# Batches 2 and 3 of an attention: keys and queries transposed by VectorE in 32x32 blocks in place of TensorE

## The chip, the cores and the metric

The kernel runs on one core of one Trainium2 chip. The metric is the time of one execution on the device in microseconds (us). The engines are TensorE (PE; its weight load is PEld), VectorE (DVE), ScalarE (ACT), GpSimd (POOL) and SyncE (SP), which issues nearly all transfers. Each engine works through its own queue in order. Sixteen data engines move what SP issues.

## The reference

A sparse attention, and then a block that mixes by Fourier transforms and applies a dense layer of two matrices. All is float32. The attention, cut to what matters here:

```python
batch, n_heads, seq, head_dim = (4, 8, 768, 64)
k_sum = k.reshape(B, H, nb, block, D).max(axis=3)          # block = 32, nb = 24
scores_l = scale * np.matmul(q, k.transpose(0, 1, 3, 2))
mask_l = np.abs(pos[:, None] - pos[None, :]) < window      # window = 16
scores_s = scale * np.einsum('bhsd,bhnd->bhsn', q, k_sum) + np.log(block)
# softmax over [scores_l where mask_l, scores_s], times [v, mean of v over each block]
```

Then `x`, the heads side by side (4, 768, 512), goes through `u = x + real(fft(fft(x, axis=1), axis=2))`, a normalisation of each row, and `u + relu(un @ w_ch1) @ w_ch2` with 512 x 2048 and 2048 x 512 weights (given as float64).

## The kernel before

The two heads of a pair are worked on together: a group `(b, g)` is batch `b` and head pair `g` (four groups a batch). For scores, keys and queries must stand with the head's 64 dimensions on the partitions: rows 0 to 63 for the first head, 64 to 127 for the second, and the 768 tokens along the row. These are the tiles `kt` (keys, two buffers, with 16 columns of margin on each side) and `qt` (queries).

**Loading.** `load(b, g)` (line 574) fetches the keys and the queries of a group, each as one transfer on SP, into a tile tagged `nat` (named `kn` or `qn`, four buffers, that is two groups). Tokens stand on the partitions: a partition has two neighbouring tokens for each of three blocks of 256 and for each head, in runs of 512 bytes. `gen_attention` loads three groups ahead (`n3`), once the group one ahead has been prepared.

**Preparing.** `prepare(b, g)` (line 678) turns these tiles. For batches 1 to 3 each tile takes six TensorE transposes of 128x128 through `ident` (line 699) into two PSUM tiles `qk`, and four ScalarE copies (line 701) of 64 partitions x 384 that write every second column of `kt` or `qt`. Then VectorE takes the maxima of the 24 blocks of keys into `km` (line 706).

**Attention.** `scores` (line 765) multiplies `kt` and `qt` block by block into `sc`, ScalarE takes the exponential (line 771), VectorE applies the mask `near`. `sum_scores` (line 781) does the same against `km`. `values` (lines 788 to 810) multiplies with the values `vw` (loaded by `load_narrow_values` as four transfers of 64 partitions, in runs of 256 bytes) and divides.

**The dense part.** `gen_hidden(b, c)` runs the first matrix in a seven-product scheme: for each of eight `j`, products into the banks `hx`, `hy`, `hz` (line 1268), gathered in `h` by ScalarE copies and VectorE sums (all VectorE sums have line 566, as they go through the helper `tt`). `gen_out` does the second matrix (lines 1310 and 1333). The weights are converted once during batch 0 (tile `words`), kept in HBM as `dw1` and `dw2`, and fetched again for each later batch (`w<-dw`). In batch 1, `get_w2` fetches four parts of each of the first four `w2` tiles, builds the other three by VectorE sums (`w<-w`), and stores them.

**Order.** The attention of batch `b + 1` is woven into the dense part of batch `b`: `drive` advances the generators `most` and `gen_attention(b + 1)` in a fixed ratio, and the scheduler then fixes each engine's queue from priorities and modelled times. The last group's preparation of batch 1's attention is that of group (2, 0). `marks["dense"]` is the dense VectorE sum that was emitted last, and

```python
with tc.issue_after(marks["dense"]):
```

puts what is emitted inside behind it in VectorE's queue. `fetch` keeps SP's queue in program order only while `in_order[0]` is true, which ends before batch 0's dense part.

Of the kernel before, what the change touches and what calls it, by code (L numbers as in the profile page):

```python
# [490 lines left out]
def _main_program(ctx, tc, q, k, v, moe_w_ch1, moe_w_ch2, out):  # L491


    nc = tc.nc
    B, H, S, D = q.shape
# [55 lines left out]
    def fetch(out, in_):  # L551

        ins = nc.sync.dma_start(out=out, in_=in_)
        if in_order[0]:
            tc.keep_in_program_order(ins)

    def abank(shape, name):
        return psum.tile(shape, FP, tag="attn", bufs=4, name=name)

    def bank(shape, name):  # L560
        return psum.tile(shape, FP, tag="bank", bufs=4, name=name)
# [10 lines left out]
    nat, marks = {}, {}  # L572

    def load(b, g, *which):

        for n in which or (1, 0):
            t = nat[b, g, n] = apool.tile([P, 2, NST // 2, 2 * D], FP, tag="nat", bufs=4, name=f"{'qk'[n]}n_{b}_{g}")
            fetch(out=t.rearrange("p e j n -> p (e j) n"),
                  in_=(q, k)[n][b, 2 * g:2 * g + 2].rearrange("e (j p s) d -> p (e j) (s d)", p=P, s=2))

# [97 lines left out]
    def prepare(b, g, *which):  # L678
        qn, kn = (nat[b, g, n] for n in range(2))
        kt, km = kt_bufs[g % 2], km_bufs[g % 2]  # L680
        qt = apool.tile([P, S], FP, tag="qt", name=f"qt_{b}_{g}") if 0 in (which or (0,)) else None
        for n in which or (1, 0):
            src, dst = (kn, kt[:, W:W + S]) if n else (qn, qt)
            if is_wide(b):
                for j0, j1 in ((0, 2), (2, 3)):
                    n = 2 * P * (j1 - j0)
                    ps = bank([P, n], f"qk_{b}_{g}_{j0}")
                    for j in range(j0, j1):
                        for s in range(2):
                            for e in range(2):  # L690
                                nc.tensor.matmul(ps[D * e:D * (e + 1), 2 * P * (j - j0) + s:2 * P * (j - j0 + 1):2],
                                                 src[:, e, j, D * s:D * (s + 1)], ident, start=True, stop=True)
                    nc.scalar.copy(out=dst[:, 2 * P * j0:2 * P * j1], in_=ps)
            else:
                for e in range(2):

                    ps = abank([P, S2], f"qk_{b}_{g}_{e}")
                    for j in range(NST // 2):
                        nc.tensor.transpose(ps[:, P * j:P * (j + 1)], src[:, e, j, :], ident)  # L699
                    for s in range(2):  # L700
                        nc.scalar.copy(out=dst[D * e:D * (e + 1), s:S:2], in_=ps[D * s:D * (s + 1)])
        if which == (0,):
            nat[b, g] = qt
            return
        with tc.issue_after(marks["fold", 0]) if (b, g) == (1, 0) else ExitStack():
            nc.vector.tensor_reduce(out=km[:, 0:nb], in_=kt[:, W:W + S].rearrange("p (n f) -> p n f", f=BLOCK),
                                    op=ALU.max, axis=AX.X)
        nat[b, g] = qt
# [110 lines left out]
    def first_attention():  # L819
# [3 lines left out]
        wt["fold"] = split_fold(0, fold)  # L823
        p = {0: wide_scores(0, 0, lambda: add_blocks(0))}
        prepare(0, 1)
        sum_values(0, 0)
        load(0, 3)
        for g in range(NP - 1):
            p[g + 1] = wide_scores(0, g + 1, (lambda: add_blocks(1)) if g == 1 else None)
            wide_values(0, g, p[g], x)  # L830
            load_values(*following(0, g, 2))
            for par in range(2):
                fold_sequence(par, g)
            if g == 0:
                get_tables(0)
            if g < NP - 2:
                prepare(0, g + 2)
                sum_values(0, g + 1)
            if g == NP - 3:
                load_raw(1)  # L840
                load(1, 0)
                load_raw(2)
                sum_values(0, g + 2)
# [105 lines left out]
    def gen_attention(b):  # L949
# [3 lines left out]
        for g in range(NP + 1):  # L953
# [26 lines left out]
            if n1 and b == 1:  # L980
                prepare(*n1)
            elif n1:
                prepare(*n1, 1)
                for _ in range(pause // 2):
                    yield
                prepare(*n1, 0)
            if n3:
                load(*n3)
# [400 lines left out]
    for vw in vw_bufs:  # L1389
        nc.gpsimd.tensor_copy(out=vw[:, :, D].rearrange("p (e n) -> p e n", e=2),  # L1390
                              in_=count[:, None, :].to_broadcast([P, 2, NQ]))
# [115 lines left out]
```

## Time and profile before

| | |
|---|---|
| median of three runs | 814.2 us (813.47 to 815.4) |
| the profiled execution | 820.64 us, its span 818.8 us |
| mean granted TensorE clock | 0.981 |
| TensorE busy | 793.2 us, 97% |
| VectorE busy | 492.6 us, 60% |
| ScalarE busy | 252.0 us, 31% |
| GpSimd busy | 46.2 us, 6% |
| SP's transfer queue (q1) | 100992 packets, 118.52 MB, 50.2% of 16 engines |

The profile is one execution, taken by the hardware profiler, 6.4 us above the median of the runs without it. The page gives for each engine the busy time, then the span in 40 slices of 20.5 us with the busy tenths of each (and the granted clock of TensorE, PEclk), then the chain of work that ended last, followed back from the last instruction. The groups name line, engine, operation, output and inputs with their shape, the count, busy time, mean duration, and the idle time of the engine just before them with what ended it. "issue" is time in which an engine waited for nothing that the profile shows. The share of the data engines can exceed 1[...].

### The profile page before, as it was taken

What the parts mean: (1) busy time and instruction counts of PE and PEld (TensorE: products, weight loads), DVE (VectorE), ACT (ScalarE), POOL (GpSimd) and SP (SyncE); (2) the same over time, 40 slices, a digit from 0 to 9 for tenths busy, and PEclk for the clock granted to TensorE, in tenths of its full rate; (3) what the DMA queues carried; (4) which work ended last, traced back from release to release, by engine and by line L of the source; (5) the groups of instructions that cost most, each with busy time, mean ns of one, the idle gap of its engine ahead of it and who ended that gap; (6) DMA issues with size and microseconds to landing.
All of it is one profiled execution on the core that took longest, in us unless ns stands there. A gap on an engine that the chain in (4) does not pass through costs nothing.

```text
span 818.8 us, 14635 instructions
## 1 busy us (share of the span) xinstructions
PE 793.2 (97%) x5998; PEld 581.6 (71%) x5998; DVE 492.6 (60%) x1121; ACT 252.0 (31%) x549; POOL 46.2 (6%) x85
## 2 busy tenths in 40 slices
PE   8969899999999999999999999999999999999997
PEld 6768665545579865688669876688659875786686
DVE  5767999887997753453577723364566723532351
ACT  3523765543635132411126114320116202001200
POOL 0010000000000310000030300000120000000000
PEclk9959999999999998999999999999999999999999
DMA  9998699788734376744614256411614044205001
GB/s 201 229 207 172 161 311 295 169 260 249 248 135 145 116 256 157 169 116 103 251 42 149 78 194 185 92 47 35 243 39 152 26 160 163 90 1 224 1 27 54
DMA packets 102332, 121.85 MB, mean 149 GB/s; under 512 B 50768, under 2 KB 83760, under 8 KB 102064
## 3 DMA queue, kind: packets, MB, share of 16 engines
q1 hardware_dynamic: 100992, 118.52, 50.2%
q0 software_dynamic: 576, 2.10, 0.8%
q8 instruction: 49, 0.80, 0.4%
q10 hardware_dynamic: 688, 0.20, 0.1%
q14 instruction: 27, 0.22, 0.1%
HBM read 97.22 MB, written 23.59 MB: 148 GB/s over the span
## 4 chain that ended last, share of the span: by engine, by line
PE 89%; DVE 4%; ACT 3%; DMA 2%; issue 1%; SPq 0%; DVEq 0%
PE hx L1268 20%; PE ox L1333 17%; PE hz L1268 10%; PE oz L1333 8%; PE o L1310 5%; PE hy L1268 5%; PE oy L1333 4%; PE y L1168 4%; PE sc L765 2%; PE mx L1127 2%; PE unt L1246 1%; PE av L798 1%; PE qk L699 1%; PE av L803 1%; PE ss L781 1%; DMA words<-in_v_dram 1%
## 5 line engine op out<-in xcount | busy, mean ns | idle before, releaser
L1268 PE MATMUL hx<-u,w 128*128 128x384 f32 x512 | 187.1, 493 | 0.3 <-ACT h L1279 0.2
L1268 PEld LDWEIGHTS hx<-u,w 128*128 128x128 f32 x512 | 95.1, 191 | 68.1 <-issue 3.6
L1268 PE MATMUL hz<-u,w 128*128 128x384 f32 x256 | 93.8, 489 | 0.0
L1333 PE MATMUL oz<-w,s 128*128 128x256 f32 x336 | 80.8, 379 | 0.0
L1333 PE MATMUL ox<-w,s 128*128 128x256 f32 x336 | 80.3, 380 | 0.0
L1333 PE MATMUL ox<-w,h 128*128 128x256 f32 x336 | 79.0, 380 | 1.0 <-DVE x L566 1.0
L566 DVE TENSOR_TENSOR x<-ox,x 128x256 f32<-128x256 f32 x84 | 35.2, 422 | 68.5 <-PE ox L1333 68.1
L1268 PEld LDWEIGHTS hz<-u,w 128*128 128x128 f32 x256 | 48.9, 192 | 34.6 <-issue 1.1
L1333 PEld LDWEIGHTS ox<-w,h 128*128 128x128 f32 x336 | 63.1, 190 | 10.5 <-DVE x L566 1.4
L1333 PEld LDWEIGHTS ox<-w,s 128*128 128x128 f32 x336 | 63.0, 190 | 9.9 <-issue 1.2
L1333 PEld LDWEIGHTS oz<-w,s 128*128 128x128 f32 x336 | 63.4, 190 | 8.7 <-DVE x L566 0.3
L1279 ACT COPY h<-hx 128x384 f32<-128x384 f32 x32 | 15.3, 479 | 143.1 <-PE hx L1268 143.0
L566 DVE TENSOR_TENSOR h<-hx,h 128x384 f32<-128x384 f32 x32 | 17.8, 555 | 55.7 <-PE hx L1268 55.7
L566 DVE TENSOR_TENSOR h<-hy,h 128x384 f32<-128x384 f32 x32 | 17.8, 555 | 50.1 <-PE hy L1268 48.1
L1268 PE MATMUL hy<-u,w 128*128 128x384 f32 x128 | 47.0, 488 | 0.6 <-issue 0.6
L1310 PE MATMUL o<-w,h 128*128 128x512 f32 x96 | 42.3, 595 | 0.0
L771 ACT ACTIVATE p<-sc 128x384 f32<-128x384 f32 x24 | 10.7, 488 | 95.1 <-PE sc L765 77.4
L1333 PE MATMUL oy<-w,h 128*128 128x256 f32 x168 | 39.9, 379 | 0.0
L1295 ACT ACTIVATE h<-hx 128x384 f32<-128x384 f32 x32 | 15.7, 491 | 70.1 <-PE hx L1268 70.0
L1268 PEld LDWEIGHTS hy<-u,w 128*128 128x128 f32 x128 | 24.0, 190 | 17.2 <-issue 1.2
L566 DVE TENSOR_TENSOR x<-oz,x 128x256 f32<-128x256 f32 x42 | 17.7, 422 | 30.1 <-PE oz L1333 29.8
L1333 PEld LDWEIGHTS oy<-w,h 128*128 128x128 f32 x168 | 31.9, 190 | 4.3
(162 smaller groups left out, 1147.1 us busy)
## 6 DMA issues: line engine op xcount, KB each, us to landing
w<-dw SPq DMA_DIRECT2D x44, 896.0 KB, 5.6
words<-in_moe_w_ch_dram SPq DMA_DIRECT2D x32, 512.0 KB, 6.1
dw<-w SPq DMA_DIRECT2D x12, 896.0 KB, 7.2
vw<-in_v_dram SPq DMA_DIRECT2D x47, 192.0 KB, 5.8
kn<-in_k_dram SPq DMA_DIRECT2D x16, 384.0 KB, 5.5
qn<-in_q_dram SPq DMA_DIRECT2D x16, 384.0 KB, 6.5
out_dram<-x SPq DMA_DIRECT2D x24, 256.0 KB, 2.5
vb<-in_v_dram SPq DMA_DIRECT2D x24, 192.0 KB, 4.2
```

Source lines behind the costliest of these rows:

```text
L566: return nc.vector.tensor_tensor(out=out, in0=in0, in1=in1, op=op).ins
L699: nc.tensor.transpose(ps[:, P * j:P * (j + 1)], src[:, e, j, :], ident)
L765: nc.tensor.matmul(ps[h][r:r + 64, i, :], kt[rows, o:o + 64], qt[rows, o:o + BLOCK], start=True, stop=True)
L771: nc.scalar.activation(out=p[:, h], in_=ps[h], func=AF.Exp, scale=SC)
L781: nc.tensor.matmul(ps[r:r + 32, :], km[rows, :], qt[rows, S2 * h:S2 * (h + 1)], start=True, stop=True)
L1127: nc.tensor.matmul(out, y[:, g], table, start=False, stop=True, skip_group_check=True)
L1168: nc.tensor.matmul(y, fgs[b][par][:, st, P * g:P * (g + 1)], fs[par][:, g % 2, st, :], start=(st == 0), stop=(st == n - 1))
L1268: ins = nc.tensor.matmul(ps, w[:, a, kk, :], u[:, r, kk, :], start=start and kk == 0, stop=stop and kk == 1, skip_group_check=True)
L1279: nc.scalar.copy(out=c11, in_=X)
L1295: nc.scalar.activation(out=c21, in_=X, func=AF.Relu)
L1310: nc.tensor.matmul(ps, h[:, n, hf, P * t:P * (t + 1)], wt[2, b, j][:, 2 * hf:2 * hf + 2, :], start=(n, hf) == (0, 0), stop=(n, hf) == (NC ...
L1333: nc.tensor.matmul(ps, left[a][:, n, :], wt[2, b, j][:, r, :], start=start and n == 0, stop=stop and n == NC - 1, skip_group_check=True)
```

## The change

For batches 2 and 3 the `nat` tile is read as 24 pieces of 32 columns in each partition. Each load becomes four transfers, one for each group of 32 partitions (head `e`, half `h` of its dimensions): partition `r + p` gets, for each of the 24 blocks of 32 tokens, the 32 dimensions of that half of token `p` of the block, a run of 128 bytes. One VectorE instruction over 128 x 768 then transposes every 32x32 block in place of the six TensorE transposes and the four ScalarE copies, and writes `kt` or `qt` directly. It is put behind the dense sum emitted last. Batches 0 and 1 keep their way, and the maxima of the keys stay as they are.

```diff
@@ load
             t = nat[b, g, n] = apool.tile([P, 2, NST // 2, 2 * D], FP, tag="nat", bufs=4, name=f"{'qk'[n]}n_{b}_{g}")
+            if b > 1:
+                t = nat[b, g, n] = t.rearrange("p e j n -> p (e j n)").rearrange("p (m c) -> p m c", c=32)
+                for e in range(2):
+                    for h in range(2):
+                        r, o = D * e + 32 * h, (q, k)[n][b, 2 * g + e].offset + 32 * h
+                        fetch(out=t[r:r + 32], in_=bass.AP((q, k)[n].tensor, o, [[D, 32], [32 * D, S // 32], [1, 32]]))
+                continue
             fetch(out=t.rearrange("p e j n -> p (e j) n"),
                   in_=(q, k)[n][b, 2 * g:2 * g + 2].rearrange("e (j p s) d -> p (e j) (s d)", p=P, s=2))
@@ prepare
             src, dst = (kn, kt[:, W:W + S]) if n else (qn, qt)
+            if b > 1:
+                with tc.issue_after(marks["dense"]):
+                    nc.vector.transpose(out=dst, in_=src.rearrange("p m c -> p (m c)"))
+                continue
             if is_wide(b):
```

## The prediction

> **What bounds the kernel now.** I read the page's busy times and slices first, then the chain in order of time, then groups by shape, then the same stretches for the data engines. Columns of the first view: busy us, share of the span, instructions; then tenths per slice of 20.5 us.
>
> ```profile
> PE 793.2 (97%) x5998; PEld 581.6 (71%) x5998; DVE 492.6 (60%) x1121; ACT 252.0 (31%) x549; POOL 46.2 (6%) x85
> ...
> PE   8969899999999999999999999999999999999997
> ...
> DVE  5767999887997753453577723364566723532351
> ...
> PEclk9959999999999998999999999999999999999999
> DMA  9998699788734376744614256411614044205001
> ```
>
> TensorE is full from end to end at full clock. VectorE and the data engines are near full only in the first third; the groups that the change touches are prepared at 163 us and from 300 us on.
>
> The chain in order of time (start, us, what), around two of those groups:
>
> ```profile
> 311.91 1.65 issue
> 313.56 1.50 PE sc L765 x47
> ...
> 316.50 2.86 PE hx L1268 x4
> ...
> 323.73 1.29 PE hy L1268 x4
> 325.02 0.66 PE qk L699 x6
> 325.68 1.29 PE hx L1268 x4
> 326.97 1.29 PE hz L1268 x4
> 328.26 0.66 PE qk L699 x6
> 328.92 1.29 PE hx L1268 x4
> ```
>
> The transposes (qk, L699) stand in the chain without a gap on either side: TensorE's queue is the clock here, and each six of them costs 0.66 us. The groups by shape (columns: busy us, mean ns, idle before) give their number and what follows them:
>
> ```profile
> L701 ACT COPY kt<-qk 64x384 f32<-64x384 f32 x48 | 24.3, 506 | 31.9 <-PE qk L699 31.1
> L701 ACT COPY qt<-qk 64x384 f32<-64x384 f32 x48 | 24.2, 504 | 2.8 <-PE qk L699 2.1
> L706 DVE TENSOR_REDUCE km<-kt 128x24 f32<-128x768 f32 x16 | 15.2, 948 | 7.0 <-ACT kt L701 6.8
> L699 PE MATMUL qk<-ident,kn 128*128 128x128 f32 x72 | 11.2, 288 | 2.2 <-DVE wide L566 2.0 <-ACT kt L701 0.2
> L699 PE MATMUL qk<-ident,qn 128*128 128x128 f32 x72 | 10.9, 286 | 0.7 <-DVE x L566 0.4 <-ACT kt L701 0.2
> ```
>
> 72 each for batches 1 to 3, so 48 and 48 go. The mean of 288 ns is a pipelined matmul from end to end; the path pays 0.66/6 = 0.109 us. Last, the stretches (busy us of PE, PEld, DVE, ACT, POOL; clock; data engine share; GB/s) and one row of the waits:
>
> ```profile
> 309.50:313.00 3.50, 2.41 (x124) 2.14 (x114) 0.73 (x2) 0.00 (x0) 0.00 (x0) 1.00 1.16 273
> 313.00:320.00 7.00, 6.44 (x61) 3.62 (x61) 3.56 (x11) 1.36 (x3) 0.00 (x0) 0.53 0.55 67
> 355.00:363.00 8.00, 8.00 (x230) 6.68 (x215) 4.39 (x12) 1.26 (x3) 0.00 (x0) 1.00 0.57 102
> 368.00:378.00 10.00, 10.00 (x55) 8.92 (x53) 4.69 (x9) 4.00 (x8) 0.00 (x0) 1.00 0.27 79
> ```
>
> ```profile
> DVE w L566 <- DMA w<-dw: 6.7, 3, 2.9
> ```
>
> The 1.65 us stop at 311.91 falls where the data engines are saturated (1.16), and for the next 7 us the clock is 0.53: the scores took 1.50 where 0.66 is usual, sums 1.43 for 0.78, hx 2.86 for 1.29, hz 1.80 for 1.29. That is 3.6 us on top of 1.65.
>
> [...] Half it is here, but after 1.65 us; gaps of 0.86 and 0.56 us (at 544.85 and 525.27 in the chain) cost no clock. [...] The page agrees (queue q8, instruction: 49 packets, 0.80 MB), so I read the stop, which waits for no semaphore, as a late fetch; that it was late because the data engines were full is inference.
>
> **The change, part by part.**
>
> *Removed, TensorE:* 16 tiles x 0.66 us = 10.5 us, all of it on the path, since the matmul behind starts at once. This is the gain. Below that it can only fall if TensorE waits for something new.
>
> *Removed, ScalarE:* 64 copies x 0.50 = 32 us, hidden before (ScalarE 31% busy) and worth nothing; four PSUM borrowings per group go too, and no wait of a matmul in 230 to 590 us names them.
>
> *Added, VectorE:* 16 transposes of 128x768. No such row exists. [...] I take 1.0, like the reduction: 16 us in all[...]. Cover: VectorE is busy 53 of 114 us in 296 to 410 and 34 of 78 in 482 to 560. Scores of the group start at 334.96, queries are now ready at 330.7, keys' maxima at 328.4; a transpose straight from SBUF replaces TensorE plus a 2.06 us train of copies[...]. Behind it on VectorE stand the dense sums that free PSUM; a delay of 1 us is less than the 2.99 us that VectorE idles before the sum at 325.13. If that cover fails, TensorE waits the excess. The one tile pair at 163 us meets a VectorE that is 90% busy: 2 us of weight conversion come later, behind stock that TensorE has not waited for after 140 us.
>
> *Changed, loads:* 8 issues for a group where 2 stood. Pieces of 128 bytes: 2 x 3072 = 6144 a group, before 1536 of 512 bytes. Their price from two clean stretches: 355 to 363 holds only four vw loads, 3072 pieces of 256 bytes, 0.57 x 8 = 4.56 us of all 16 engines, so 23.8 ns a piece and engine; 368 to 378 only one kn and one qn, 1536 of 512 bytes, 2.7 us, 28.1 ns. Along that line 128 bytes cost 21.6 ns. [...] I take 22 (21 to 28): 384 pieces an engine x 22 = 8.4 us a group (8.1 to 10.8), **5.7 more than before**. Loads run about 45 us ahead of use, so their own landing is hidden. The three at 101, 135 and 169 us land in the weight stage, where the engines are near full; a few us there are in front of conversions that hold a lead.
>
> *SP queue:* a vw issue of as many pieces took 0.65 us (2.28 when blocked), kn 0.38. Eight times 0.65 less two times 0.38: 4.4 us a group, up to 8 when blocked. Behind it stand the fetches of w2 (302.86, 303.95) and of vw (309.71). The vw fetch has 20 us of slack. The w2 fetches of batch 1 do not: VectorE waited 2.87 us for one until 312.24.
>
> *Crowding:* from 296 to 410 the data engines' busy time adds up to 71 us; four groups x 5.7 add 23, a third more. The three late fetches of TensorE cost 1.65 + 3.6 + 0.86 + 0.56 = 6.7 us in the seven groups from 300 to 560. In proportion to the load that grows by 2.1 us (0 to 7; below nothing, if that one stop moves away, -5).
>
> **Sum:** -10.5 + 2.1 = -8.4 us against the profiled run's 820.6 (span 818.8, 1.8 around it): 812.2. That run lies 6.4 above the median of 814.2, which becomes **806** after rounding.
>
> **The rivals.**
>
> *A, the forecast* (0.52): TensorE shrinks by its transposes and little comes back. Own range 799 (all 10.5 and most of the stop at 311.91 gone) to 812.
>
> *B, the crowd blocks VectorE* (0.33): in batch 1's hidden layer (296 to 333 us) each of four w2 tiles is fetched, summed by VectorE and stored. VectorE works in order; if its sum waits for a fetch that now lies behind eight small-piece loads, 5.7 us pass in which no PSUM bank is freed, reciprocals and masks behind it too, and TensorE stops after its free banks are spent. A stop of that length is followed by the half clock: 5.7 + 3.6 = 9.3 us at most for each. For it: the wait is there already, in the fullest stretch. Against it: TensorE did not stop for that wait, and has about 4.5 us of attention work in it that needs none of those banks (0.17 + 1.13 + 0.87 + 1.53 + 0.78 us in the chain). One such stop leaves 813; from the second it decides: -10.5 + 18.6 = 8 slower, 822; three give 832. The price of a piece would decide too: at 40 ns a group loads for 15 us of its 23.
>
> *C, TensorE waits for VectorE instead* (0.15): the transposes are queued behind a dense sum, so scores come late by what was saved, about 1.3 us a group; the time is then 813 to 818. For it: TensorE's order is fixed ahead. Against it: 4 us lie between the queries and their scores.
>
> That the change does not do what it says would be transposes split in many instructions[...].
>
> **How the numbers follow.** A is faster whole; B is slower whole; C is 0.09 within 0.2% (1.6 us, about what a measurement can tell here from no change) and 0.06 slower. So 0.52, 0.09, 0.39. The range 799 to 826 takes in A, C and the nearer part of B; some 0.15 stay outside, most of it above. A alone has 799 to 812.
>
> **What would show it.** In the profile after: 48 qk matmuls of each kind left and 32 copies each; 16 new VectorE rows of about 1.0 us; kn and qn issues four times as many for batches 2 and 3; the hidden rows untouched at 1.29 us per four. Right: no longer waits of TensorE between 296 and 410. Wrong: "DVE w" waiting for its fetch by far more than 6.7 us, more "issue" pieces in the chain, more slices below full clock, or a transpose row over 2 us.

## The result and the profile after

The change costs time: median 853.2 us (851.22 to 856.08) against 814.8 (813.47 to 816.66) for the kernel before in the same comparison, a ratio of 1.047 (95% interval 1.0447 to 1.0494). The profiled execution took 856.08 us, its span 854.3, 35.5 more than that of the kernel before.

The first view, of the changed kernel (columns as above, slices of 21.4 us):

```profile
PE 794.4 (93%) x5902; PEld 577.1 (68%) x5902; DVE 506.1 (59%) x1137; ACT 221.5 (26%) x485; POOL 46.6 (5%) x85
...
PE   8969998979966999899999999999999999999997
...
DVE  4768977748599775355457754454375933442352
...
PEclk9969898999987999999999999999999999999999
```

TensorE's busy time is about what it was; the added 35 us are idle or slow. Most of them lie in slices 9 to 13 (about 171 to 278 us): VectorE falls to 4 tenths in slice 9, TensorE to 6 in slices 12 and 13, with the clock down there too. That is batch 0's dense part with the conversion of the weights. Of the groups that the change deals with, only (2, 0) is transposed in it, at 155.6 us; the next one follows after the stage, once batch 1's dense part has begun.

So I cut each execution at the same instructions: from the first `ss` product after 100 us to the first transpose (`unt`) of batch 1's Fourier part, from there to that of batch 2, to the last row of these transposes in batch 3, and to the end (us). The last column adds up TensorE's stops ahead of scores ("PE sc" released by "issue") from 264 to 660 us, as the view of the waits gives them.

| | before it | weights, batch 0 | batch 1 | batches 2, 3 | end | stops |
|---|---|---|---|---|---|---|
| before | 111.8 | 154.5 | 183.8 | 190.4 | 178.2 | 2.5 |
| after | 112.2 | **186.7** | 187.2 | 190.6 | 177.5 | 9.1 |
| e1, late groups only | 105.4 | 154.6 | 184.8 | 184.3 | 177.5 | 3.4 |
| e2, early groups only | 107.5 | 188.4 | 190.0 | 188.2 | 178.2 | 5.1 |
| e3, small loads, TensorE transposes | 110.4 | 158.6 | 187.9 | 192.3 | 177.9 | 4.0 |
| e4, old loads, VectorE transposes | 109.5 | 152.7 | 183.1 | 193.1 | 179.2 | 11.6 |
| e5, four transfers of 512-byte runs | 109.4 | 172.0 | 184.4 | 195.9 | 177.5 | 11.6 |
| e6, queues of after, 512-byte runs | 111.8 | 190.1 | 186.0 | 189.1 | 177.6 | 7.8 |
| e7, queues of before, 128-byte runs | 110.8 | 154.6 | 187.8 | 190.6 | 178.2 | 4.1 |
| e8, conversions given priority | 111.0 | 196.8 | 183.4 | 189.2 | 177.5 | 9.1 |
| e9, loads issued by ScalarE | 116.4 | 164.4 | 183.3 | 197.6 | 178.2 | 12.1 |
| e10, loads issued by GpSimd | 110.9 | 157.0 | 193.1 | 196.7 | 178.3 | 19.7 |
| e11, e10 with loads behind scores | 102.8 | 155.4 | 179.7 | 195.2 | 178.1 | 9.9 |
| e12, e1 with loads behind scores | 106.6 | 154.5 | 180.4 | 191.6 | 177.4 | 2.6 |

Of the 35.5 us, 32.2 are in the weight stage. The work in it is not quite the same in all rows: in after, e2, e3, e5 and e6, 14 products of the second matrix come behind its end that come ahead of it in the others. Four such products take 0.86 us in the kernel before (at 633.28), so by this estimate these five lose 3 us more in the weight stage than the table says (below: at equal work) and 3 less in batch 1; in e9 the start of the stage falls at other work too. The stretch before it differs by several us between executions, in kernels whose queues up to the end of the weight stage are the same too (before 111.8, e12 106.6), so the stages say more of a single execution than its span. They repeat well: the four kernels that share the order of before in that stage (before, e1, e7, e12) take 154.5 to 154.6 us for it, the three that share that of after (after, e2, e6) 186.7 to 190.1.

The groups by shape, of after, show the part that was forecast:

```profile
L717 DVE TENSOR_REDUCE km<-kt 128x24 f32<-128x768 f32 x16 | 15.1, 945 | 3.5 <-ACT kt L712 3.5
L693 DVE STREAM_TRANSPOSE kt<-kn 128x768 f32<-128x768 f32 x8 | 7.8, 969 | 0.0
L693 DVE STREAM_TRANSPOSE qt<-qn 128x768 f32<-128x768 f32 x8 | 7.7, 964 | 0.0
L710 PE MATMUL qk<-ident,kn 128*128 128x128 f32 x24 | 4.6, 318 | 3.3 <-DVE fold L566 3.1 <-ACT kt L712 0.2
```

One VectorE instruction a tile, 0.97 us like the reduction, no idle time before it, and 48 of 72 `qk` matmuls of each kind gone. So the change does what it says; the cost is elsewhere.

The waits from 95 to 300 us in after (us in total, times, longest):

```profile
DVE vs L566 <- PE vs L799: 14.1, 1, 14.1
PE hx L1279 <- DVE w L566: 9.3, 2, 5.9
PE oy L1344 <- DVE w L566: 4.8, 2, 3.0
PE o L1321 <- DVE w L566: 4.5, 1, 4.5
```

None of these four stood in the kernel before. The longest one in VectorE's timeline, the last weight piece and what comes next (start, us, instruction, idle before and its releaser), of before and then of after, and the piece of after's chain beside it:

```profile
182.61 0.68 DVE L1034 SCALAR_TENSOR_TENSOR words<-words 128x512 f32<-128x512 uint32 x1
183.21 0.28 DVE L566 TENSOR_TENSOR vs<-vs,half 128x128 f32<-128x128 f32 x1
```

```profile
166.00 0.69 DVE L566 TENSOR_TENSOR w<-words 128x512 f32<-128x512 f32 x1
180.77 0.29 DVE L566 TENSOR_TENSOR vs<-vs,half 128x128 f32<-128x128 f32 x1 [14.09 <-PE vs L799]
```

```profile
156.53 24.03 PE o L1321 x56
180.57 0.17 PE vs L799 x2
```

VectorE stands idle for 14 us with weights left to convert, because the next instruction in its queue is an attention sum whose operand TensorE makes only after 56 products of the second matrix. TensorE makes that operand at much the same time in both kernels (from 180.40 us in after, from 181.42 in before); but in before VectorE has more conversions ahead of the sum and comes to it at 183.21, with no wait, where in after it is there at 166.7. The words' buffers come free late, so SP fetches late, in after:

```profile
SPq L553 <- DVE words L1045: 36.6, 5, 17.4
SPq L553 <- DVE words L1039: 18.1, 2, 17.2
```

Single waits of 17 us, where the longest for `words` in the kernel before was 9.8. Then TensorE waits for weights, the rows "<- DVE w". The stage from 170 us to its end, by stretches (columns as in the prediction), of before and then of after:

```profile
170.00:266.00 96.00, 95.81 (x462) 63.74 (x462) 82.56 (x195) 44.00 (x101) 0.74 (x1) 1.00 0.62 199
```

```profile
170.00:299.00 129.00, 106.99 (x460) 68.72 (x459) 94.19 (x219) 48.84 (x109) 0.74 (x1) 0.91 0.59 173
```

TensorE has 0.2 us free of 96 before, 22 of 129 after, and its busy time grows by 11 as the clock falls to 0.91.

The order itself is the scheduler's, and it changed. In VectorE's queue 21 of the 32 converted pieces (`w<-words`) stand ahead of the last `vs` sum of the weight stage before, 15 after; of TensorE's 96 `o` products, 68 stand ahead of its `vs` before, 56 after. (The expectation of e8 counts eight earlier sums on `words` too, so 29 and 23 of 40, and takes two `o` products as one, 34 and 28.) What made it do so is what the experiments ask.

### The profile page after: what moved, and what is told of

The parts are those of the page before. It is cut to its first block, busy times and chain, and to the rows that moved or that the text cites. A ratio compares the mean times of both kernels' runs of the same rounds, so it can differ in the third digit from the quotient of the medians.

```text
span 854.3 us, 14415 instructions
## 1 busy us (share of the span) xinstructions
PE 794.4 (93%) x5902; PEld 577.1 (68%) x5902; DVE 506.1 (59%) x1137; ACT 221.5 (26%) x485; POOL 46.6 (5%) x85
## 4 chain that ended last, share of the span: by engine, by line
PE 81%; DVE 10%; DMA 3%; issue 2%; ACT 2%; SPq 1%; ACTq 0%; DVEq 0%
PE hx L1279 18%; PE ox L1344 16%; PE hz L1279 9%; PE oz L1344 8%; PE o L1321 5%; PE hy L1279 5%; PE oy L1344 4%; PE y L1179 3%; DVE w L566 2%; PE sc L776 2%; PE mx L1138 2%; PE av L809 2%; PE av L814 1%; PE unt L1257 1%; SPq L553 1%
## 5 line engine op out<-in xcount | busy, mean ns | idle before, releaser
L1279 PE MATMUL hx<-u,w 128*128 128x384 f32 x512 | 190.5, 500 | 9.7 <-DVE w L566 9.3
L1279 PEld LDWEIGHTS hx<-u,w 128*128 128x128 f32 x512 | 97.2, 194 | 81.3 <-DVE w L566 10.5
L1279 PE MATMUL hy<-u,w 128*128 128x384 f32 x128 | 49.2, 509 | 0.0
L782 ACT ACTIVATE p<-sc 128x384 f32<-128x384 f32 x24 | 10.6, 488 | 105.4 <-PE sc L776 105.4
L1321 PEld LDWEIGHTS o<-w,h 128*128 128x128 f32 x96 | 18.7, 197 | 27.9 <-issue 22.1
```

Source lines behind the costliest of these rows:

```text
L782: nc.scalar.activation(out=p[:, h], in_=ps[h], func=AF.Exp, scale=SC)
L1279: ins = nc.tensor.matmul(ps, w[:, a, kk, :], u[:, r, kk, :], start=start and kk == 0, stop=stop and kk == 1, skip_group_check=True)
L1321: nc.tensor.matmul(ps, h[:, n, hf, P * t:P * (t + 1)], wt[2, b, j][:, 2 * hf:2 * hf + 2, :], start=(n, hf) == (0, 0), stop=(n, hf) == (NC ...
```

## The experiments

Ratios are against the kernel before on the same chip, with the 95% interval.

**Which groups.** e1 applies the change to the five groups loaded after the weight stage, e2 to the three others.

```diff
-            if b > 1:                # in load and in prepare
+            if (b, g) > (2, 2):      # e1
+            if b == 2 and g < 3:     # e2
```

> The change only for the five groups that are loaded after the weight stage: (2, 3) and batch 3. Theory 1 (the whole loss arises in batch 0's dense part, where weights are fetched and converted): 32.5 of the 35.5 us vanish; 5/8 of the saved TensorE time, 6.6 us, stand against some 3 us of new waits in batch 1's dense part, so 808 to 816 us, and the tokens' transposes of batch 1 (unt) start within 3 us of before (266). Theory 2 (the loss comes with each group alike): 5/8 of 38, so some 838.

> The change only for the three groups (2, 0), (2, 1), (2, 2), loaded beside the weights. Theory 1: the loss is whole, 845 to 852 us, unt of batch 1 starts near 299. Theory 2 (each group alike): 3/8 of 38, some 829.

e1: 811.4 us, 0.995 [0.9931, 0.9969]. e2: 857.2 us, 1.054 [1.0481, 1.0599]. e2 lies 5 us above its range, and above the whole change too. Three groups bring the whole loss, and they bring it in the weight stage (188.4), where two of them are only loaded; in e2 the next is transposed at 333 us, 37 us after that stage. The queues of that stage in e2 are those of after, instruction for instruction, and in e1 those of before. In e1 ten tiles less on TensorE shorten batches 1 to 3 from 374.2 to 369.1 us: 5.1, where 10 x 0.66 = 6.6 was the forecast rate. TensorE's busy time in them falls by 6.9 us (369.5 to 362.6), and its free time grows by 1.8.

**Which half of the change.** e3 keeps the TensorE transposes and splits each load in four with 128-byte runs; e4 has the VectorE transposes and each load as one transfer in 512-byte runs, so its blocks hold other tokens than the score products ask for. (The code here and below is shortened.)

```diff
+                for c in range(0, 2 * D, 32):        # e3: columns c to c + 32 of both sides
+                    fetch(out=...[:, :, c:c + 32], in_=...[:, :, c:c + 32])
```

> Only the loads are cut: batches 2 and 3 keep the layout and the TensorE transposes of before, but each tile is fetched by four transfers in runs of 128 bytes (as many pieces as the change has: 3072 a tile). Theory A (the small pieces hold SP's queue and the data engines and the weights come late): slow like the change or more, since TensorE saves nothing, 845 to 865 us. Theory B (VectorE's transposes and the order of queues that goes with them make the loss): within 5 us of before, 813 to 820.

> Only the transposes are changed: VectorE transposes as in the change, but each tile is loaded as before by one transfer with runs of 512 bytes, so the keys and queries of batches 2 and 3 stand in a wrong order (the numbers are not the reference's, the work is the same). Theory A: faster than before by nearly the 10.5 us of TensorE, 803 to 808 us. Theory B: slow, 840 to 853.

e3: 828.8 us, 1.0177 [1.0124, 1.023]. e4: 819.3 us, 1.0057 [1.0034, 1.008]. Both lie between the ranges of their two theories: neither half makes the 38 us. e3 has as many issues on SP as the change, in as small pieces, and still its weight stage is only 4.1 us longer than before (7 at equal work). e4 is also the first surprise the other way: no TensorE transposes, no small pieces, and no gain. Its weight stage is 1.8 us shorter, but batches 2 and 3 are 2.7 us longer and the stops ahead of scores rise from 2.5 to 11.6 us.

**Pieces or issues.** e5 is e4 with each load in four transfers of 512-byte runs, by partition groups.

> The changed kernel with four transfers a tile in runs of 512 bytes, written so that the scheduler knows it (keys and queries of batches 2 and 3 stand in a wrong order, the work is the same). Theory C: the scheduler's order depends on the time that it gives the loads; with these it places the conversions in another order than in the change, so the time is off the change's, 812 to 835 us. Theory A: the same as the kernel with exchanged patterns, 805 to 818. If the count of transfers is what the scheduler reacts to, near the change, 845 to 853.

e5: 840.9 us, 1.0306 [1.0252, 1.0359], between the ranges again. With no small piece at all the weight stage goes from 152.7 to 172.0 (e4 to e5), only because four transfers stand where one stood. In its waits VectorE stands 8.5 us at one `x` sum for an `o` product: another order, the same kind of fault.

**Order or load.** Here the queues are held and only the patterns of the transfers are exchanged, after the scheduler is done. e6 has the queues of after with 512-byte runs; e7 has the queues of before, TensorE transposes and one transfer a tile, but in 3072 runs of 128 bytes. Both read other data into the tiles than the score products ask for.

```diff
+    if is_small_load(ins):                     # e6: four transfers a tile as in the change
+        ins = replaced(ins, out=[[768, 32], [128, 6], [1, 128]])
+    if is_load_of_batch_2_or_3(ins):           # e7: one transfer a tile
+        ins = replaced(ins, out=[[768, 128], [32, 24], [1, 32]])
```

> The changed kernel with every engine's queue exactly as the scheduler left it, and only the access patterns of the small loads exchanged afterwards: the same four transfers for a tile, in runs of 512 bytes in place of 128 (768 pieces a tile and not 3072; keys and queries of batches 2 and 3 stand in a wrong order, the work is the same). Theory A (the small pieces hold the data engines and SP): back to 805 to 818 us. Theory C (the order that the scheduler made of VectorE's and TensorE's queues in batch 0's dense part makes the loss): 840 to 853 us, with VectorE still waiting some 14 us for the sums' matmul vs.

> The kernel before with every queue exactly as it was, TensorE transposes and all, and only the access patterns of the 16 loads of batches 2 and 3 exchanged afterwards: one transfer a tile as before, but in 3072 runs of 128 bytes (the order of the numbers within a tile is wrong, the work is the same). Theory A: the loads' 5.7 us a group more of the data engines cost dearly beside the weights, 830 us or more. Theory C: 813 to 820 us.

e6: 852.3 us, 1.0435 [1.0388, 1.0481]. e7: 822.9 us, 1.0082 [1.0042, 1.0122]. This separates the pieces from the rest: the order (with its four issues a tile) without the pieces keeps the loss, weight stage 190.1, and the longest of VectorE's waits in the stage is the one of after:

```profile
DVE vs L566 <- PE vs L799: 15.9, 1, 15.9
```

The pieces without the order cost 0.8% (2.9 us above the range) and leave the weight stage at 154.6. What e6 can't tell apart, the order and the longer row of issues on SP, e3 helps with: there the same issues and pieces stand in SP's queue, but VectorE has 19 conversions ahead of the `vs` sum (21 before, 15 after) and waits nowhere for `vs`, and the stage is 7 us longer at equal work where after's is 35. What else differs is who transposes the tiles, and that costs the stage nothing in e4. So most of the 35 us is the order's.

**Repairing the order by priority.** In e8 the conversions get a priority bonus.

```diff
-            drive((most, 5, 0), (weights, 15, 0), (attn, 1, 0))
+            drive((most, 5, 0), (weights, 15, 600), (attn, 1, 0))
```

> The change as it is, but the weight conversions of batch 0's dense part are driven with a priority bonus of 600, so that the scheduler puts 30 of the 40 conversions ahead of the last values sum of batch 1's first attention groups in VectorE's queue (29 in the kernel before, 23 in the changed one) and 34 second-matrix products ahead of it on TensorE (34 before, 28 after). Theory that the order of the queues is the cause: the stage of the conversions goes back from 187 us to about 155 to 160, and the kernel from 853 to 815 to 826. Rival, that the four transfers a tile and the transposes cost time where they stand, whatever the order: 845 to 853. Rival, that another engine's order was what counted (values and masks of the attention are now too late): between, 830 to 845.

858.1 us, 1.0516 [1.0465, 1.0568], weight stage 196.8: worse, and the first theory as I had put it falls. VectorE now waits only 1.2 us for `vs`, but TensorE waits for VectorE:

```profile
PE o L1321 <- DVE h L566: 21.2, 1, 21.2
```

A dense sum came to stand behind the conversions, which VectorE works off without a pause from 135 to 161 us at least, while TensorE is idle from 150.7 to 171.8. The number of conversions ahead of one instruction is a symptom, not a dial. What seems to count is that the queues of VectorE and TensorE fit each other.

**Taking the transfers off SP.** e10 issues the small loads from GpSimd, e9 from ScalarE; pieces, bytes and transposes stay.

```diff
-                        fetch(out=t[r:r + 32], in_=...)
+                        nc.gpsimd.dma_start(out=t[r:r + 32], in_=...)     # e10; nc.scalar in e9
```

> The change as it is, but the 64 small loads of batches 2 and 3 are issued by GpSimd instead of SP. All the pieces, bytes and transposes stay; SP's queue has two transfers fewer a group than in the kernel before, not six more. The scheduler then leaves the order as it was (30 conversions ahead of the last values sum, 34 second-matrix products ahead of it on TensorE). Theory that the transfers in SP's queue make the scheduler reorder the weight stage: that stage goes back to about 155 us, and the whole to 805 to 818. Rival, that the small transfers themselves crowd the data engines: the loss stays, over 840. Rival, that GpSimd's issuing is slow and the loads land late: stops of TensorE for qn or kn, 825 to 840 with the conversion stage still near 155.

> The change as it is, but the 64 small loads of batches 2 and 3 are issued by ScalarE instead of SP. SP's queue is as short as with GpSimd, but VectorE's and TensorE's order is another one: no second-matrix product stands ahead of the last values sum of TensorE (34 before, 28 after), and the next group's maxima of keys stand behind 20 to 28 conversions instead of 13 to 27. Theory that the order alone counts: not the old 155 us, but some 160 to 175 for the conversion stage, the whole 820 to 840. Theory that SP's longer queue itself counts: as with GpSimd, 805 to 818. Rival, that the small transfers crowd the data engines: over 840.

e10: 836.4 us, 1.0261 [1.0193, 1.0328]. e9: 841.3 us, 1.0317 [1.0272, 1.0362]. The weight stage of e10 is 157.0, so 29.7 of its 32.2 us come back with every small transfer in place and the transposes on VectorE. e9, with another order, lies between at 164.4, VectorE waiting 9.3 us at `vs` in two waits. In e10 the order of the weight stage is back near that of before (22 conversions and 68 `o` products ahead of `vs`), as the first mechanism has it. But e10's total lies 18 us above its range, since its two later stages lose 9.3 and 6.3 us against before. The total is in the range of the rival with late landings, but no wait of TensorE in those stages names `kn` or `qn`. The chain names where. Pieces of "issue" over 3 us in e10 from 260 us on:

```profile
311.64 4.43 issue
...
336.68 5.50 issue
...
512.96 3.09 issue
...
535.52 3.81 issue
```

And around the second one, three stretches:

```profile
331.00:336.70 5.70, 5.68 (x194) 4.37 (x193) 3.25 (x9) 0.49 (x1) 4.79 (x8) 1.00 0.94 181
336.70:342.20 5.50, 0.02 (x3) 0.01 (x3) 0.00 (x0) 0.00 (x0) 0.00 (x0) 0.71 1.20 219
342.20:348.00 5.80, 5.80 (x36) 3.06 (x36) 1.03 (x2) 1.84 (x4) 0.00 (x0) 0.69 0.59 67
```

194 matmuls in 5.7 us, then 5.5 us in which no engine works and the data engines are full (1.20), then the clock at 0.69. GpSimd issued this group's eight loads from 328.6 to 334.7. The stop at 311.91 in the kernel before is of this form: 1.65 us with the data engines at 1.16, then the clock at 0.53.

**Moving the loads away from the scores.** e11 is e10 with each load waiting until VectorE has masked the scores of the group before, by way of a copy of one column of each tile (14 copies); e12 does the same to e1.

```diff
+            with tc.issue_after(masked):          # the mask sum in scores
+                for n in range(2):
+                    nc.vector.tensor_copy(out=spare[:, n:n + 1], in_=nat[b, g, n][:, 0, 0:1])
...
+            if late:                              # after sum_scores
+                load(*late)
```

> As e10 (the small loads issued by GpSimd), but a group's loads now wait for the scores of the group before it: VectorE copies one column of the two loaded tiles right behind its mask sum, and the tiles' buffers come free only then (14 small copies more; no other engine's queue changes). With e10 TensorE stopped for 19.7 us ahead of scores (sc, released by nothing the profile shows) between 264 and 660 us, and the stages of batches 1 and 2 took 193 and 197 us where 184 and 190 were usual. Theory, that these stops are late instruction fetches behind the group's own small loads, which start 5 to 8 us before them: stops fall below 8 us, the two stages to 184 to 189 and 189 to 192, the whole to 818 to 826. Rival, that the stops come from TensorE's dense run of small score products alone, whatever is in flight: stops of 15 to 20 us, 832 to 840. Rival, that the delayed loads now land late: VectorE waits for kn and qn, over 836.

> The change for the five groups loaded after the weight stage alone, as in e1, and their loads put behind the scores of the group before as in e11 (10 small copies more). Queues until the end of batch 0's dense part are those of the kernel before. e1 took 811.4 (0.995 of the kernel before) with 3.4 us of stops ahead of scores between 264 and 660 us. Theory, that loads in flight ahead of the scores make the stops: stops under 2 us, 806 to 811, ratio 0.988 to 0.995. Rival, that place and number of the stops don't depend on it: as e1 or a few us longer, since the later queues come out otherwise, 810 to 818.

e11: 815.8 us, 0.9995 [0.9975, 1.0015]. TensorE's, ScalarE's and SP's queues are those of e10, VectorE's has the copies more and GpSimd's the loads at other places, and 20.6 us of median are gone, which is 2 us better than the range. (Of the 24.7 us between the two profiled spans, 14.8 lie in batches 1 to 3 and 8.1 in the stretch ahead of the weight stage, where nothing was changed.) The stops halve, from 19.7 to 9.9 us (forecast: under 8); batch 1's stage falls by 13.4 to 179.7 (forecast: 184 to 189). Batches 2 and 3 keep 195.2 where 189 to 192 was expected, with stops of 5.5 us left in them: half confirmed. e12: 812.5 us, 0.9959 [0.9943, 0.9976], no better than e1, as its rival had it. Its stops are 2.6 us (forecast: under 2), but its later queues came out differently, so it tells little. e1 and e12 are the fastest here, half a per cent ahead of the kernel before.

## Why the prediction was wrong

**The step that failed** is the one on the three early loads: "a few us there are in front of conversions that hold a lead", and the 2 us of conversion that come "behind stock". It priced 18 more transfers as work inserted into queues that otherwise stay. They don't: my own description says that the scheduler fixes each queue from modelled times, so an edit to one queue can be an edit to all. The term was near nothing and measured 32.2 us (35 at equal work), shown by e1 and e2 (where), e5 and e6 (issues and order, not pieces), e7 (pieces alone), e3 (issues and pieces in nearly the old order: 7) and e10 (back to 157 when SP doesn't carry them). It should have been a rival with a price: VectorE has 83 us of work in the 96 us from 170 to 266 before, so, as an estimate from that row, each us of VectorE waiting beyond 13 is a us of the kernel.

**Two sizes were off.** *Pieces:* forecast 5.7 us more of the data engines for a group. The transfer queue's share, of after and of e7, then of e6:

```profile
q1 hardware_dynamic: 138624, 118.53, 50.7%
```

```profile
q1 hardware_dynamic: 137856, 118.52, 53.5%
```

```profile
q1 hardware_dynamic: 101760, 118.53, 49.6%
```

Between after and e6, of equal queues, this is 433.1 - 423.9 = 9.2 us over eight groups, 1.2 for each; between e7 and before (50.2% of 818.8) it is 28.7, or 3.6 for each. The price taken from the line through 256 and 512 bytes was too dear by a factor of 1.6 to 5. The packets themselves, one by one in the trace, say it more directly: those of 128 bytes took 15.4 ns in the mean in after, where the forecast put 22, so 5.9 us a group for 8.4. Three quarters of them took 13 ns or less, where nine tenths of the 256-byte packets took 18 or more. *Crowding:* forecast +2.1 us (0 to 7). The stops ahead of scores went from 2.5 to 9.1 us, not counting the clock's fall behind some of them, so the upper end was needed, but not for the reason given: e4, with the loads of before, has 11.6. When the loads start decides as much as how many pieces they have, as e10 against e11 shows.

**What was right.** The transpose, 1.0 us forecast and 0.97 measured, its cover intact. The issues: 2.14 and 2.25 us for four at 337.5 us, so 3.6 more for a group, 4.4 forecast. The gain of TensorE, 5.1 of 6.6 us where the order of the weight stage stays (e1). In after batches 1 to 3 nevertheless take 377.8 us where 374.2 stood. Some 3 us of this are the 14 products that came over from the weight stage. For the rest TensorE is busy less (365.6 us, 369.5 in the kernel before; 3 less still without those products), but free for 7.6 us more, 6.7 of them stops ahead of scores: the gain is used up by the stops. The clock is no part of it: it was at half for 6.8 us in both, in the kernel before behind the stop of 1.65 us, in after for 3.4 us each behind the stops of 4.2 and 1.9 us and behind none of the four of 0.6 to 0.9 us. (The prediction's list has 48 `qk` matmuls of each kind and 32 copies left; these are the numbers that go, and 24 and 16 are left.)

**The rivals.** A's gain was not to be seen in the total. B's wait went the other way: VectorE's wait for the fetches of batch 1's `w2` tiles fell from 6.7 to 1.1 us, and one of 2.4 us for a store of `x` is new. B had the sign, but for a different place and cause, so that was luck. C did not occur: no wait of a score for a transpose. None of the three had an order that changes ahead of the edit. Of the signs of being wrong, more pieces of "issue" and more slices below full clock came; a longer wait of "DVE w" for its fetch and a transpose over 2 us did not.

**Open:** which modelled time makes the scheduler choose the worse order when four transfers replace one; and why batches 2 and 3 take 195 to 198 us in e5, e9, e10 and e11, of which the stops explain a part.

## What to carry to other kernels

Where a scheduler orders the queues from a model, count the instructions that an edit adds to each queue and compare the queues before and after, over the whole kernel and not only at the edit: here the loads of three groups reordered a stage that ended before two of them were used. When the loss shows as an engine idle in front of one instruction, ask first what stands behind it in the queue. And treat the start of a prefetch as a choice: set off behind the dense run of small matmuls and not in front, it paid in e11 (20.6 us of median against e10; in e12 the gain did not show).

## What the runs showed of the hardware that was not expected

- Runs of 128 bytes are cheap here: 15.4 ns each on their engine, where those of 512 bytes took 31.4 in the kernel before. e7 moves the tiles of batches 2 and 3 in 3072 of them, with a median of 6.1 and 7.3 us to landing for all keys and all queries, where with 768 runs of 512 bytes throughout it was 5.5 and 6.5.
- TensorE stops for up to 5.5 us with nothing to wait for in the records, after 194 matmuls in 5.7 us and with the data engines at 1.20 (e10). In e10 these stops take 19.7 us, and moving loads alone halves them, to 9.9 in e11. All eight stops of over half a us ahead of scores between 264 and 660 us in the kernel before and in after end 1.2 to 1.7 us after a packet of queue q8 does (on the page "instruction": 49 packets in 0.80 MB before, 48 in 0.79 MB after), and an execution has only these 49 or 48 in over 800 us. That TensorE waits for the instructions in such a packet is my inference, and so is that the packet comes late because the data engines are full; neither was shown.
- The stretch ahead of the weight stage took 111.8 us in the kernel before and 106.6 in e12, with the same queues. In slices 2 and 3 of the page, from 20 to 61 us, the data engines are at 9 tenths or more in both, but move 229 and 207 GB/s in the kernel before and 222 and 261 in e12; why isn't settled.
